# Row maxima of an attention kernel: a quarter of the tile pairs through a ScalarE Relu, the maxima turned by way of DRAM, and the output product in one piece

## The chip, the cores and the metric

The kernel runs on one core of a Trainium2 chip. The metric is device time in microseconds (us). The core has five engines that run side by side and wait for each other through semaphores: TensorE (PE in the profile, its weight loads PEld), VectorE (DVE), ScalarE (ACT), GpSimd (POOL) and SyncE (SP), which here only issues DMAs. Matmuls write to PSUM banks of 128 x 512 float32; VectorE and ScalarE read those banks, GpSimd does not.

## The reference, cut to what matters

```python
x = A_x                                                    # 2048 x 512, 32 heads of 16
mod = silu(c) @ w_mod                                      # six rows: sa, ca, ga, sb, cb, gb
h = layernorm(x) * (1 + ca) + sa
q = (h @ wq) as 32 heads; k = h @ wk; v = h @ wv           # one k and one v for all heads
p = softmax(q k^T * 16 ** -0.5)
x = x + ga * ((p v) as 2048 x 512 @ wo)
h = layernorm(x) * (1 + cb) + sb
x = x + gb * ((sigmoid(h @ w_gate) * (h @ w_up)) @ w_down)
```

The softmax is over 2048 keys for each of 32 x 2048 rows. The kernel subtracts each row's exact maximum before the exponential, so it needs the scores twice: once to find the maxima, once to exponentiate.

## The kernel before, in words

Queries come in four blocks `b` of 512, and a unit is four heads of one block: 32 units, numbered `i`. A unit has 16 steps (`kb`), one per 128 keys; `s = 16 i + kb` counts all 512 steps.

In a step `scores(n)` is called for n = 0 to 3, one head each. It issues two things. `st_tile` multiplies 128 keys by 512 queries into a PSUM bank of the tag `st` (two banks), and ScalarE takes the exponential of it into the tile `P`. `a_tile` multiplies 128 queries by 512 keys into a bank of the tag `sa` (three banks), 76 tiles ahead (`A0`, so about 19 steps, for the next unit), and VectorE reduces it to one maximum per row, in `mx`. In scores(n) the `a_tile` is that of head `n ^ 1`. A unit has 64 such tiles: 4 heads, 4 blocks `qt` of 128 queries, 4 blocks `kc` of 512 keys. The two matmuls of one scores(n) use different halves of TensorE's rows.

`pv` adds the product of the step two before (`LAG`) to the bank `c`: four matmuls with 32 columns of `V` each, in float32. In a step without feed-forward work it comes in two halves of 256 queries, one after scores(1), one after scores(3); with feed-forward work it comes whole after scores(1).

The steps of the first eight units carry, between scores(0) and scores(1), pieces of the query projection (`light`, tile `pq`: 24 pairs of matmuls over 17 steps, so one or two pairs a step, up to step 121). From unit 8 on, `plan` hands out pieces of the feed-forward layer of the block before (tiles `po`, `pgu`, `pd`), four to five pairs of matmuls per step, placed after scores(0), scores(2) and scores(3). A few steps get none.

When a unit's 64 tiles are done, `max_end`, called three steps before the unit's first scores, reduces `mx` to 16 columns (tile `m`), `max_rows` turns them on TensorE into a bank of the tag `sa`, ScalarE copies and scales that, GpSimd splits it into a high and a low float16 (`mh`), and four DMAs write it into two rows of the query tile `qp`. A constant in the key tile `kp` makes the score matmul subtract the maximum. In unit 0 the order of tiles is by blocks of queries, the maxima are turned a block at a time, and `parts` lets its steps work on one such block.

From the first step on the program order on TensorE, VectorE and ScalarE is the written order (`keep`, through `Ordered`, once `pinned` is set); GpSimd and SyncE are ordered by a scheduler. Before the first step (the prologue) the scheduler orders all engines, from the list `PLAN`.

Of the kernel before, what the change touches and what calls it, by code (L numbers as in the profile page):

```python
# [28 lines left out]
EPS = 1e-5  # L29
SH = 4.0  # L30
SW = 16.0
SM = 16.0

PLAN = 'n1 x2 l0 k0 x3 t1 l3 e1 w0 l1 n2 w3 k1 w1 q00 n3 q01 t2 t3 e2 e3 l2 m a1 k2 a2 k3 a4 w2 a8 p z3 a12 z4 a16 z2 a18 z5'

E32 = [(0, 1), (1, 1), (2, 0), (3, 3), (3, 1)]
ELO = [(0, 3), (0, 1), (3, 1), (3, 2), (2, 1), (3, 0), (1, 1)]
# [3 lines left out]
LAG = 2  # L43
# [16 lines left out]
PBUFS = 4  # L60
SBANKS = {"st": 2, "sa": 3}
GWB = 3
HBUFS = 36


@with_exitstack
def adaln_mqa_glu_kernel(
# [15 lines left out]
    pool, sp = nc.gpsimd, nc.sync  # L83
# [6 lines left out]
    cp = ctx.enter_context(tc.tile_pool(name="cp", bufs=1))  # L90
# [12 lines left out]
    def sbank(name):  # L103
        return psum["s"].tile([P, 512], F32, tag=name, name=name, bufs=SBANKS[name]) if "s" in psum else bank(name)
# [13 lines left out]
    pinned = []  # L118
# [46 lines left out]
    def t32(name, shape=(P, 512)):  # L165
        return wp.tile(list(shape), F32, tag="f32", name=name, bufs=18)
# [152 lines left out]
        dve.scalar_tensor_tensor(lo, w_, SW, hi, op0=ALU.mult, op1=ALU.subtract)  # L319


    kp = cp.tile([P, S], F16, name="kp")
    V = cp.tile([P, NKB, 32], F32, name="V")
    dve.memset(V, 1.0)
    qD = dr.tile([2, D, S], F16, name="qD")
# [58 lines left out]

# [28 lines left out]
    mxs = {}  # L413
# [3 lines left out]
    Cs = {}  # L417
# [22 lines left out]
        return qps[b, o], 2 * (u % 2)  # L440


    def a_tile(i, n):
        qp, pr0 = get_q(i)
        if i not in mxs:
            mxs[i] = wp.tile([P, 4, 4, 4], F32, tag="mx", name="mx", bufs=2)
        h = n % 4
        kc, qt = (n // 4 % 4, n // 16) if i == 0 else (n // 16, n // 4 % 4)
        j, pr = heads[h]
        sa = sbank("sa")  # L450
        pe.matmul(sa, qp[64 * j:64 * j + 64, pr0 + pr, qt * P:(qt + 1) * P],  # L451
                  kp[64 * j:64 * j + 64, kc * 512:(kc + 1) * 512], start=True, stop=True)
        dve.tensor_reduce(mxs[i][:, 2 * j + pr, qt, kc:kc + 1], sa, axis=AX.X, op=ALU.max)  # L453
        if i == 0 and n % 16 == 15:
            pend.append((i, n // 16, n // 16 + 1))
        elif i > 0 and n == 63:
            pend.append((i, 0, 4))

    pend = []

    def max_end(i, t0, t1):
        nt = t1 - t0
        n = 4 * nt
        m16 = wp.tile([P, n], F32, tag="m16", name="m16", bufs=4)
        dve.tensor_reduce(m16.rearrange("p (h t) -> p h t", t=nt), mxs[i][:, :, t0:t1, :], axis=AX.X, op=ALU.max)
        return lambda: max_rows(i, t0, t1, m16)

    def max_rows(i, t0, t1, m16):
        qp, pr0 = get_q(i)
        nt = t1 - t0  # L470
        n = 4 * nt
        pm = sbank("sa")
        pe.transpose(pm[:n, :P], m16, ident)
        mh = wp.tile([n, 2, P], F16, tag="mh", name="mh", bufs=4)
        if pinned:
            m32 = wp.tile([n, P], F32, tag="m32", name="m32", bufs=4)
# [3 lines left out]
        else:  # L480
            dve.tensor_scalar(mh[:, 0], pm[:n, :P], 1.0 / SM, None, op0=ALU.mult)
            dve.scalar_tensor_tensor(mh[:, 1], pm[:n, :P], 1.0 / SM, mh[:, 0],
                                     op0=ALU.mult, op1=ALU.subtract)
        for j in range(2):
            for h in range(2):
                r = 64 * j + 48 + h
                sp.dma_start(qp[r:r + 1, pr0:pr0 + 2, t0 * P:t1 * P], mh[2 * nt * j:2 * nt * (j + 1), h, :])


    def parts(i, t):  # L490
        if i == 0:
            return [(4 * (t % 4) + n, slice(n * P, (n + 1) * P), slice(t // 4 * P, (t // 4 + 1) * P)) for n in range(4)]
        return [(t, slice(0, QB), slice(0, QB))]

    def st_tile(i, t, pr, j):
        qp, pr0 = get_q(i)
        if j == 0:
            P_["p"] = P2.tile([P, 2, 512], F32, tag=f"P{pr}", name=f"P{pr}", bufs=PBUFS)
        p_ = P_["p"]
        s_ = sbank("st")  # L500
        for kb, cols, qs in parts(i, t):
            pe.matmul(s_[:, cols], kp[64 * j:64 * j + 64, kb * P:(kb + 1) * P],
                      qp[64 * j:64 * j + 64, pr0 + pr, qs], start=True, stop=True)
        act.activation(p_[:, j], s_, AF.Exp, scale=0.25)
        Ps[i, t, 2 * pr + j] = p_[:, j]

    def pv(i, t, half=None):
        if t == 0 and half != 1:  # L510
            Cs[i] = cbank("c")
        ps = parts(i, t)
        if half is not None:
            if i == 0:
                ps = ps[2 * half:2 * half + 2]
            else:
                cut = slice(half * QB // 2, (half + 1) * QB // 2)
                ps = [(t, cut, cut)]
        for kb, cols, qs in ps:
            for hh in range(4):  # L520
                pe.matmul(Cs[i][32 * hh:32 * hh + 32, qs], V[:, kb, :], Ps[i, t, hh][:, cols],
                          start=(kb == 0 and (i == 0 or half != 1)), stop=(kb == NKB - 1 and (i == 0 or half != 0)))
        if half == 0:
            return
        for hh in range(4):
            del Ps[i, t, hh]
        if t == NKB - 1:
            unit_end(i)
# [271 lines left out]

    for tok in PLAN.split():
        f_, args = tok[0], [int(tok[1:])] if tok[0] == "a" else [int(z) for z in tok[1:]]
        if f_ == "n":
            ln1_norm(*args)
        elif f_ == "t":
            for k in range(NDC):
                ln1_tr(args[0], k)
        elif f_ == "e":
            ln1_block(*args)
        elif f_ == "k":  # L810
            kv_block(*args)
        elif f_ == "q":
            q_group(*args).alone()
        elif f_ == "w":
            split_wq(*args)
        elif f_ == "l":
            load_wq(*args)
        elif f_ == "x":
            load_x(*args)
        elif f_ == "a":  # L820
            emit_a(4 * args[0])
        elif f_ == "m":
            for i in (4, 3, 2, 5):
                load_mod(i)
        elif f_ == "z":
            mod2(*args)
        elif f_ == "p":
            max_end(*pend.pop(0))()
    emit_a(A0)
    pctx.close()  # L830
    psum["ctx"].close()
# [95 lines left out]
    for i, (b, u) in enumerate(units):  # L927
# [4 lines left out]
        for kb in range(NKB):  # L932
# [3 lines left out]
            for z in [z for z in waits if z[0] <= s]:  # L936
                waits.remove(z)
                z[1]()
            rows = [max_end(*z) for z in late]
            an = A0 + 4 * s  # L940

            def scores(n):
# [87 lines left out]
```

## Time and profile before

| | |
|---|---|
| median of 3 runs | 1740.58 us (1739.97 to 1740.6) |
| the profiled execution | 1740.14 us, its span 1738.4 us |
| TensorE, VectorE, ScalarE, GpSimd busy | 1691.9, 1443.2, 1226.3, 605.1 us |
| prologue, up to the first exponential | 115.3 us |
| units 0 to 31, to the last exponential | 115.3 to 1590 us |
| last block's feed-forward layer | the rest, to 1738.4 us |

Times within the profile are us from the start of the span. A group's row has, after its shapes and count, the busy time, the mean ns of one, and the engine's idle time just before them. A merged row of the timeline has its start, its length, the engine, the line, the operation and how many.

Matmul ends are modelled, so starts are the better mark: a matmul that starts late has waited.

### The profile page before, as it was taken

The numbers are of one execution on the slowest core, as the hardware profiler recorded it, in microseconds if no ns is written. First come the engines' busy times: TensorE is split into PE (matmuls) and PEld (weight loads), VectorE is DVE, ScalarE is ACT, GpSimd is POOL, SyncE is SP. The second block draws the span as 40 slices with busy tenths as digits, with TensorE's granted clock in tenths as the row PEclk, the third lists the DMA queues.
The fourth block names the chain that finished last, engine by engine and source line by source line (L and its number), as shares of the span: only waits on it lengthen the run. The fifth ranks groups of instructions, "written<-read, shape, count | busy, mean of one in ns | idle before, by whom it ended". The sixth has DMA issues, their size and how long they took to land.

```text
span 1738.4 us, 35892 instructions
## 1 busy us (share of the span) xinstructions
PE 1691.9 (97%) x14467; PEld 591.1 (34%) x14467; DVE 1443.2 (83%) x2407; ACT 1226.3 (71%) x2231; POOL 605.1 (35%) x715
## 2 busy tenths in 40 slices
PE   5889999999999999999999999999999999999998
PEld 3335333333233333333333333333333333333443
DVE  8889999999998988888899898988898888841311
ACT  3338888888878777777778777777778777774100
POOL 4131445454443332332245232233255141231433
PEclk9769999999999999999999999999999999999999
DMA  7111223231100110111111110011101010011211
GB/s 262 40 47 31 95 85 106 89 110 63 51 23 26 47 49 12 33 38 41 32 41 33 33 50 20 26 47 47 36 17 57 28 57 5 30 50 55 75 60 49
DMA packets 66238, 90.94 MB, mean 52 GB/s; under 512 B 14752, under 2 KB 41376, under 8 KB 66072
## 3 DMA queue, kind: packets, MB, share of 16 engines
q1 hardware_dynamic: 66072, 88.66, 15.6%
q8 instruction: 113, 1.85, 0.4%
q14 instruction: 53, 0.43, 0.1%
HBM read 67.68 MB, written 16.22 MB: 48 GB/s over the span
## 4 chain that ended last, share of the span: by engine, by line
PE 86%; DVE 7%; ACT 2%; POOL 1%; issue 1%; DMA 1%; SPq 0%; POOLq 0%; DVEq 0%; ACTq 0%
PE c L116 27%; PE st L116 20%; PE pgu L116 12%; PE sa L116 8%; PE pd L116 5%; PE pgu L139 4%; DVE mx L116 3%; PE pd L139 2%; PE pq L116 2%; PE po L116 2%; ACT P L116 2%; PE sa L451 1%; DVE mx L453 1%; PE pmod L222 1%; PE pt L116 1%
## 5 line engine op out<-in xcount | busy, mean ns | idle before, releaser
L116 ACT ACTIVATE P<-st 128x512 f32<-128x512 f32 x2048 | 1139.2, 595 | 283.7 <-PE sa L116 250.0
L116 DVE TENSOR_REDUCE mx<-sa 128x1 f32<-128x512 f32 x1972 | 1241.2, 684 | 113.6 <-PE sa L116 108.3
L116 PE MATMUL st<-qp,kp 64*128 64x512 f16 (+1 forms) x2240 | 746.8, 362 | 7.1 <-DVE mx L453 2.4
L116 PE MATMUL sa<-kp,qp 64*128 64x512 f16 x1972 | 725.3, 382 | 0.5 <-DVE mx L116 0.5
L116 PE MATMUL c<-P,V 128*32 128x512 f32 (+2 forms) x5552 | 577.6, 492 | 2.9 <-DVE cs L116 2.9
L116 PEld LDWEIGHTS <-kp 64*128 64x128 f16 x2240 | 187.8, 94 | 500.1 <-issue 407.2
L116 PE MATMUL pgu<-h2h,gw 64*128 64x512 f16 x1344 | 242.6, 376 | 0.0
L116 PEld LDWEIGHTS <-qp 64*128 64x128 f16 x1972 | 181.8, 93 | 137.0 <-issue 51.9
L116 PEld LDWEIGHTS c<-P,V 128*32 128x32 f32 x5552 | 111.5, 108 | 192.1 <-issue 177.3
L727 POOL TENSOR_SCALAR th<-th 128x512 f32<-128x512 f32 x42 | 26.0, 619 | 335.8 <-ACT th L116 325.8
L116 PE MATMUL pgu<-h2l,gw 64*128 64x512 f16 x672 | 132.3, 376 | 0.0
L116 PEld LDWEIGHTS <-gw 64*128 64x128 f16 x2016 | 99.6, 94 | 80.7 <-issue 3.1
L424 POOL MEMSET qp<- 32x2048 f16 x32 | 57.6, 1798 | 49.3 <-PE st L116 41.6
L139 PE MATMUL pgu<-h2h,gw 128*128 128x512 f16 x224 | 66.8, 379 | 0.5 <-ACT h2h L283 0.5
L733 POOL TENSOR_TENSOR gl<-th,gh 128x512 f16<-128x512 f32 x56 | 64.8, 1157 | 4.7
L478 POOL TENSOR_SCALAR mh<-m 16x128 f16<-16x128 f32 (+1 forms) x34 | 9.8, 288 | 159.3 <-ACT m L116 159.0
L730 DVE SCALAR_TENSOR_TENSOR th<-th,pgu 128x512 f32<-128x512 f32 x14 | 9.6, 688 | 66.3 <-PE pgu L139 53.0
L248 POOL TENSOR_SCALAR wst<-wst 128x512 f32<-128x512 f32 x46 | 28.5, 620 | 102.1 <-DMA wst<-in_B_w_down_dram 27.1
L721 ACT ACTIVATE th<-pgu 128x512 f32<-128x512 f32 x14 | 8.4, 597 | 76.9 <-PE pgu L139 76.9
L116 DVE COPY u<-pgu 128x512 f32<-128x512 f32 x42 | 28.5, 679 | 35.7 <-PE st L116 19.8
L750 POOL TENSOR_TENSOR ot<-ot,gb 128x512 f32<-128x512 f32 x10 | 12.7, 1273 | 126.7 <-ACT ot L116 126.7
L590 POOL TENSOR_TENSOR raw<-raw,rb 128x512 f32<-128x512 f32 x15 | 19.1, 1273 | 102.7 <-DMA rb<-lD 84.1
(164 smaller groups left out, 1435.3 us busy)
## 6 DMA issues: line engine op xcount, KB each, us to landing
gw<-wD SPq DMA_DIRECT2D x56, 512.0 KB
wD<-gw SPq DMA_DIRECT2D x14, 512.0 KB
wm<-in_w_mod_dram SPq DMA_DIRECT2D x6, 1024.0 KB
qp<-qD SPq DMA_DIRECT2D x96, 64.0 KB
xall<-in_A_x_dram SPq DMA_DIRECT2D x4, 1024.0 KB
qD<-q SPq DMA_DIRECT2D x16, 256.0 KB
raw<-cs SPq DMA_DIRECT2D x128, 32.0 KB
xr<-in_A_x_dram SPq DMA_DIRECT2D x16, 256.0 KB
```

Of the source, the lines that this page charges most:

```text
L116: return (lambda *a, **k: keep(f_(*a, **k))) if pinned else f_
L139: pe.matmul(self.bank, l_, r_, start=(n == 0), stop=(n == self.n - 1))
L222: pe.matmul(p_[32 * k:32 * (k + 1)], cbc[:, k, :], wmods[i][:, k, :], start=True, stop=True)
L248: pool.tensor_scalar(w_, w_, SW, 0.0, op0=ALU.mult, op1=ALU.add)
L424: pool.memset(qp[j:j + 32], 0.0)
L451: pe.matmul(sa, qp[64 * j:64 * j + 64, pr0 + pr, qt * P:(qt + 1) * P], kp[64 * j:64 * j + 64, kc * 512:(kc + 1) * 512], start=True, stop=True)
L453: dve.tensor_reduce(mxs[i][:, 2 * j + pr, qt, kc:kc + 1], sa, axis=AX.X, op=ALU.max)
L478: pool.tensor_scalar(mh[:, 0], m32, 1.0, 0.0, op0=ALU.mult, op1=ALU.add)
L590: keep(pool.tensor_tensor(raw, raw, rb, op=ALU.mult))
L727: pool.tensor_scalar(th, th, 1.0, 1.0, op0=ALU.add, op1=ALU.mult)
L733: pool.tensor_tensor(lo, th, hi, op=ALU.subtract)
L750: pool.tensor_tensor(ot, ot, mods2['gb'], op=ALU.mult)
```

## The change

Keys are paired in two blocks of 512. For one head of the four (head `h == qt`), and for all four heads in unit 0, the first tile of a pair holds half the difference of the two blocks' scores, from a new key tile `kd`; ScalarE writes its doubled positive part to an SBUF tile `rl`; one step later VectorE adds `rl` to the second block's scores and takes the row maximum in one instruction (`tensor_tensor_reduce`), since max(a, b) = b + max(a - b, 0). The other three heads are reduced as before. `kd` is made in the prologue by ScalarE (one more copy of `pk` for each block) and GpSimd.

The maxima are no longer turned on TensorE: GpSimd scales and splits them, VectorE turns 32 x 32 blocks, one DMA writes them to DRAM (`mD`), and four DMAs read them into `qp`. All of unit 0's maxima are turned at once, after 64 tiles, so `parts` goes, and a step of unit 0 is like any other. And `pv` is issued whole, after scores(1), in every step. `PLAN` asks for the prologue's tiles in pairs.

```diff
-PLAN = '... k1 ... l2 m a1 k2 a2 k3 a4 w2 a8 p z3 a12 z4 a16 z2 a18 z5'
+PLAN = '... k1 ... l2 m a1 k2 a3 k3 a5 w2 a8 z3 a12 z4 a16 z2 a18 z5'
...
+        k32[b] = t32("k32")
+        act.activation(k32[b], pk, AF.Identity, scale=0.5 / (SH * SW))
         act.activation(kb, pk, AF.Identity, scale=1.0 / (SH * SW), bias=kbias)
...
+        if b % 2:
+            kb = kd[:, b // 2 * QB:(b // 2 + 1) * QB]
+            d_, o_ = k32.pop(b - 1), k32.pop(b)
+            pool.tensor_tensor(d_, d_, o_, op=ALU.subtract)
+            pool.tensor_scalar(kb, d_, 1.0, 0.0, op0=ALU.mult, op1=ALU.add)
+            for j in (32, 96):
+                pool.tensor_tensor(kb[j:j + DH], d_[j:j + DH], kb[j:j + DH], op=ALU.subtract)
...
     def a_tile(i, n):
...
+            pool.memset(mxs[i], LEAST)
-        h = n % 4
-        kc, qt = (n // 4 % 4, n // 16) if i == 0 else (n // 16, n // 4 % 4)
+        h, qt, g, second = n % 4, n // 8 % 4, n // 32, n // 4 % 2
+        kc = 2 * g + second
+        both = i == 0 or h == qt
+        differ = both and not second
+        keys = kd[...] if differ else kp[...]
-        dve.tensor_reduce(mxs[i][:, 2 * j + pr, qt, kc:kc + 1], sa, axis=AX.X, op=ALU.max)
+        m_ = mxs[i][:, 2 * j + pr, qt, kc:kc + 1]
+        if differ:
+            more[i, h] = r_ = wp.tile([P, 512], F32, tag="rl", name="rl", bufs=RBUFS)
+            act.activation(r_, sa, AF.Relu, scale=2.0)
+        elif both:
+            dve.tensor_tensor_reduce(junk, sa, more.pop((i, h)), 1.0, LEAST, ALU.add, ALU.max, m_)
+        else:
+            dve.tensor_reduce(m_, sa, axis=AX.X, op=ALU.max)
...
+    def max_end(i):
+        dve.tensor_reduce(m16.rearrange("p (h t) -> p h t", t=4), mxs[i], axis=AX.X, op=ALU.max)
+        pool.tensor_scalar(m16, m16, 1.0 / SM, 0.0, op0=ALU.mult, op1=ALU.add)
+        pool.tensor_scalar(mm16[:, 0], m16, 1.0, 0.0, op0=ALU.mult, op1=ALU.add)
+        pool.tensor_tensor(mm16[:, 1], m16, mm16[:, 0], op=ALU.subtract)
+        return lambda: max_rows(i, mm16)
...
-        pe.transpose(pm[:n, :P], m16, ident)
-            act.activation(m32, pm[:n, :P], AF.Identity, scale=1.0 / SM)
-            pool.tensor_scalar(mh[:, 0], m32, 1.0, 0.0, op0=ALU.mult, op1=ALU.add)
-            pool.tensor_tensor(mh[:, 1], m32, mh[:, 0], op=ALU.subtract)
-                sp.dma_start(qp[r:r + 1, pr0:pr0 + 2, t0 * P:t1 * P], mh[2 * nt * j:2 * nt * (j + 1), h, :])
+        dve.transpose(mt, mm16.rearrange("p l c -> p (l c)"))
+        sp.dma_start(mD, mt)
+                sp.dma_start(qp[r:r + 1, pr0:pr0 + 2, :].rearrange(...), src[l, j].unsqueeze(0))
...
-            full = now_ is not None
             if len(vq) >= LAG:
-                pv(*vq[0], None if full else 0)
+                pv(*vq.pop(0))
             for z in rows:
                 z()
             scores(2)
             if now_ == "run":
                 piece()
             scores(3)
-            if len(vq) >= LAG:
-                if not full:
-                    pv(*vq[0], 1)
-                vq.pop(0)
```

What this does to the order is seen at two places. The first is TensorE in a step of the early units, without a `pq` piece in it. Before, the two score pairs that follow one half of `c` are followed by the other half (a row with x2 is two of the four heads):

```order
L116 MATMUL c<-P_2439,V 32x256 x2
L116 MATMUL c<-P_2458,V 32x256 x2
L116 LDWEIGHTS kp
L116 MATMUL st<-qp,kp 128x512
L116 LDWEIGHTS qp
L116 MATMUL sa<-kp,qp 128x512
L116 LDWEIGHTS kp
L116 MATMUL st<-qp,kp 128x512
L116 LDWEIGHTS qp
L116 MATMUL sa<-kp,qp 128x512
L116 MATMUL c<-P_2439,V 32x256 x2
L116 MATMUL c<-P_2458,V 32x256 x2
```

Now `c` is 512 wide, and after the two pairs the next step's scores follow at once:

```order
L118 MATMUL c<-P_2092,V 32x512 x2
L118 MATMUL c<-P_2111,V 32x512 x2
L118 LDWEIGHTS kp
L118 MATMUL st<-qp,kp 128x512
L118 LDWEIGHTS qp
L118 MATMUL sa<-kp,qp 128x512
L118 LDWEIGHTS kp
L118 MATMUL st<-qp,kp 128x512
L118 LDWEIGHTS qp
L118 MATMUL sa<-kp,qp 128x512
L118 LDWEIGHTS kp
L118 MATMUL st<-qp,kp 128x512
```

So four score pairs (with what `pq` or feed-forward pieces lie among them) now stand in a row between two whole `c`, where before every two had a half of `c` behind them.

The second place is ScalarE in the same units (`P0` holds the exponentials of scores(0) and (1), `P1` those of scores(2) and (3)). Before there are exponentials only:

```order
L116 ACTIVATE P0_2395<-st_2396 128x512
L116 ACTIVATE P0_2395<-st_2406 128x512
L116 ACTIVATE P1_2416<-st_2417 128x512
L116 ACTIVATE P1_2416<-st_2423 128x512
L116 ACTIVATE P0_2439<-st_2440 128x512
L116 ACTIVATE P0_2439<-st_2448 128x512
```

Now, in every second step, a Relu (`rl`) stands among them; here it is that of head 3, between the third exponential of a step and the fourth:

```order
L118 ACTIVATE P0_3065<-st_3066 128x512
L118 ACTIVATE P0_3065<-st_3074 128x512
L118 ACTIVATE P1_3084<-st_3085 128x512
L118 ACTIVATE rl_3090<-sa_3088 128x512
L118 ACTIVATE P1_3084<-st_3092 128x512
L118 ACTIVATE P0_3098<-st_3099 128x512
```

For heads 0, 1 and 2 it stands after the second exponential, between the first and the second, and after the fourth; so it moves the exponentials behind it on ScalarE, and the banks that they release.

More of the change, by code (lines that the diff above doesn't have):

```diff
@@ L29 @@
 EPS = 1e-5
+LEAST = -3.0e38
 SH = 4.0
@@ L62 @@
 GWB = 3
+RBUFS = 4
 HBUFS = 36
@@ L322, in adaln_mqa_glu_kernel @@
     kp = cp.tile([P, S], F16, name="kp")
+    kd = cp.tile([P, S // 2], F16, name="kd")
+    k32 = {}
+    junk = cp.tile([P, 512], F16, name="junk")
     V = cp.tile([P, NKB, 32], F32, name="V")
@@ L446, in a_tile @@
             mxs[i] = wp.tile([P, 4, 4, 4], F32, tag="mx", name="mx", bufs=2)
-        h = n % 4
-        kc, qt = (n // 4 % 4, n // 16) if i == 0 else (n // 16, n // 4 % 4)
+            pool.memset(mxs[i], LEAST)
+        h, qt, g, second = n % 4, n // 8 % 4, n // 32, n // 4 % 2
+        kc = 2 * g + second
         j, pr = heads[h]
+        both = i == 0 or h == qt
+        differ = both and not second
+        keys = kd[64 * j:64 * j + 64, g * 512:(g + 1) * 512] if differ else kp[64 * j:64 * j + 64, kc * 512:(kc + 1) * 512]
@@ L450, in a_tile @@
         sa = sbank("sa")
-        pe.matmul(sa, qp[64 * j:64 * j + 64, pr0 + pr, qt * P:(qt + 1) * P],
-                  kp[64 * j:64 * j + 64, kc * 512:(kc + 1) * 512], start=True, stop=True)
-        dve.tensor_reduce(mxs[i][:, 2 * j + pr, qt, kc:kc + 1], sa, axis=AX.X, op=ALU.max)
[L454 to L457, printed above, removed]
-    pend = []
[L461 to L466, printed above, removed]
@@ L490, in parts @@
[L490 to L493, printed above, removed]
+        pe.matmul(sa, qp[64 * j:64 * j + 64, pr0 + pr, qt * P:(qt + 1) * P], keys, start=True, stop=True)
+        m_ = mxs[i][:, 2 * j + pr, qt, kc:kc + 1]
[6 more added lines that the diff above has]
+            dve.tensor_reduce(m_, sa, axis=AX.X, op=ALU.max)
@@ new lines, in a_tile @@
+        if n == 63:
+            pend.append(i)
+    more = {}
+    pend = []
+    def max_end(i):
+        m16 = wp.tile([P, 16], F32, tag="m16", name="m16", bufs=2)
+        mm16 = wp.tile([P, 2, 16], F16, tag="mm", name="mm", bufs=2)
+        dve.tensor_reduce(m16.rearrange("p (h t) -> p h t", t=4), mxs[i], axis=AX.X, op=ALU.max)
[3 more added lines that the diff above has]
+        return lambda: max_rows(i, mm16)
@@ new lines, in max_rows @@
+    def max_rows(i, mm16):
+        qp, pr0 = get_q(i)
+        mt = wp.tile([P, 32], F16, tag="mt", name="mt", bufs=2)
+        dve.transpose(mt, mm16.rearrange("p l c -> p (l c)"))
+        mD = dr.tile([P, 32], F16, tag="mD", name="mD", bufs=2)
+        sp.dma_start(mD, mt)
+        src = mD.rearrange("(b l j r t) q -> l j r t b q", b=4, l=2, j=2, r=2)
+        for j in range(2):
+            for l in range(2):
+                r = 64 * j + 48 + l
+                sp.dma_start(qp[r:r + 1, pr0:pr0 + 2, :].rearrange("o r (t b q) -> o r t b q", t=4, b=4), src[l, j].unsqueeze(0))
@@ L500, in st_tile, with pv @@
         s_ = sbank("st")
-        for kb, cols, qs in parts(i, t):
-            pe.matmul(s_[:, cols], kp[64 * j:64 * j + 64, kb * P:(kb + 1) * P],
-                      qp[64 * j:64 * j + 64, pr0 + pr, qs], start=True, stop=True)
+        pe.matmul(s_, kp[64 * j:64 * j + 64, t * P:(t + 1) * P], qp[64 * j:64 * j + 64, pr0 + pr, :], start=True, stop=True)
         act.activation(p_[:, j], s_, AF.Exp, scale=0.25)
         Ps[i, t, 2 * pr + j] = p_[:, j]
-    def pv(i, t, half=None):
-        if t == 0 and half != 1:
+    def pv(i, t):
+        if t == 0:
             Cs[i] = cbank("c")
[L512 to L524, printed above, removed]
+        for hh in range(4):
+            pe.matmul(Cs[i][32 * hh:32 * hh + 32], V[:, t, :], Ps[i, t, hh], start=(t == 0), stop=(t == NKB - 1))
         for hh in range(4):
@@ L826, in adaln_mqa_glu_kernel @@
             mod2(*args)
-        elif f_ == "p":
-            max_end(*pend.pop(0))()
+    emit_a(64)
+    turned = max_end(pend.pop())
+    emit_a(68)
+    turned()
     emit_a(A0)
@@ L938, in adaln_mqa_glu_kernel @@
                 z[1]()
-            rows = [max_end(*z) for z in late]
+            rows = [max_end(z) for z in late]
             an = A0 + 4 * s
```

15 lines of the change are left out of this document (1 added, 14 removed).

## The prediction

> **What bounds the kernel now.** I read the busy time by stage first. The stages are the end of the prologue (75 to 115.3), unit 0, units 1 to 7 (159.1 to 451.7), and units 10 to 30 (541.2 to 1545).
>
> ```profile
> core 0: us, PE busy (x) PEld busy (x) DVE busy (x) ACT busy (x) POOL busy (x), PEclk, DMA share, GB/s
> 75.00:115.30 40.30, 34.37 (x114) 9.26 (x112) 34.86 (x63) 3.61 (x7) 9.60 (x14) 0.57 0.13 40
> 115.30:159.10 43.80, 42.65 (x811) 27.80 (x808) 40.31 (x65) 36.21 (x69) 7.14 (x12) 0.92 0.04 15
> 159.10:451.70 292.60, 288.18 (x3027) 91.91 (x3023) 285.55 (x473) 252.62 (x463) 139.21 (x172) 1.00 0.27 87
> 541.20:1545.00 1003.80, 1002.86 (x8378) 331.07 (x8376) 895.07 (x1455) 781.46 (x1426) 320.71 (x364) 1.00 0.11 36
> ```
>
> In units 1 to 7 TensorE and VectorE are both 98% busy, later TensorE 100% and VectorE 89%. The change relieves VectorE and loads ScalarE, so VectorE's share suggests a gain in the early units and none later. But TensorE's share is no less, and its busy time may contain waits. So I count steps, by the exponentials (four a step) in the same stretches of the tile P:
>
> ```profile
> core 0: us, PE busy (x) PEld busy (x) ACT busy (x), PEclk, DMA share, GB/s
> 159.10:451.70 292.60, 143.16 (x1824) 36.12 (x1824) 247.96 (x449) 1.00 0.27 87
> 541.20:1545.00 1003.80, 359.46 (x2744) 53.96 (x2744) 750.59 (x1344) 1.00 0.11 36
> ```
>
> That is 112 steps of 2.61 us early and 336 of 2.99 late. Next the timeline of one late step, which has its output product whole (c, 512 wide):
>
> ```profile
> 742.29 1.06 PE L116 MATMUL c<-P,V 128*32 128x512 f32 x8
> 743.28 0.39 PE L116 MATMUL st<-qp,kp 64*128 64x512 f16 x1
> 743.71 1.08 ACT L116 ACTIVATE P<-st 128x512 f32<-128x512 f32 x2 [0.71 <-PE sa L116]
> 743.73 0.38 PE L116 MATMUL st<-qp,kp 64*128 64x512 f16 x1
> 744.59 0.38 PE L116 MATMUL st<-qp,kp 64*128 64x512 f16 x1
> 744.84 0.37 PE L116 MATMUL st<-qp,kp 64*128 64x512 f16 x1
> 745.16 1.06 PE L116 MATMUL c<-P,V 128*32 128x512 f32 x8
> 746.16 0.39 PE L116 MATMUL st<-qp,kp 64*128 64x512 f16 x1
> ```
>
> The third st of a step starts at 743.28, its exponential 0.43 later; the two exponentials end at 744.79 (743.71 + 1.08), and the st at 744.84, the next step's second, starts 0.05 after that: with two st banks it needs the one that the fourth exponential frees. Then 0.32 to c, and 1.00 to the next st. 0.43 + 1.08 + 0.05 + 0.32 + 1.00 = 2.88, exactly the 743.28 to 746.16 of this step. So a step with a whole c is a loop through ScalarE and two banks; the feed-forward pieces merely fill the time in which TensorE would wait. An early step has c in halves:
>
> ```profile
> 256.31 0.64 PE L116 MATMUL c<-P,V 128*32 128x256 f32 x8
> 256.88 0.39 PE L116 MATMUL st<-qp,kp 64*128 64x512 f16 x1
> 257.12 0.37 PE L116 MATMUL st<-qp,kp 64*128 64x512 f16 x1
> 257.30 2.21 ACT L116 ACTIVATE P<-st 128x512 f32<-128x512 f32 x4 [0.24 <-PE sa L116]
> 257.44 0.64 PE L116 MATMUL c<-P,V 128*32 128x256 f32 x8
> 258.01 0.39 PE L116 MATMUL st<-qp,kp 64*128 64x512 f16 x1
> ```
>
> Here each half (0.57, 256.31 to 256.88) runs while ScalarE empties two banks; two scores and a half take 1.13 (256.88 to 258.01), ScalarE's two exponentials 1.08. That balance is what the change touches.
>
> **The change, part by part.** The durations that it needs:
>
> ```profile
> L116 ACT ACTIVATE P<-st 128x512 f32<-128x512 f32 x2048 | 1139.2, 595 | 283.7 <-PE sa L116 250.0 <-PE pgu L116 6.8 <-PE st L116 5.0
> L116 PE MATMUL c<-P,V 128*32 128x512 f32 x2896 | 385.5, 604 | 0.0
> L116 PE MATMUL c<-P,V 128*32 128x256 f32 x2144 | 171.3, 391 | 2.9 <-DVE cs L116 2.9
> 254.94 6.14 DVE L116 TENSOR_REDUCE mx<-sa 128x1 f32<-128x512 f32 x10
> L730 DVE SCALAR_TENSOR_TENSOR th<-th,pgu 128x512 f32<-128x512 f32 x14 | 9.6, 688 | 66.3 <-PE pgu L139 53.0 <-ACT th L721 13.3
> L116 DVE TENSOR_REDUCE m<-mx 128x4 f32<-128x16 f32 x3 | 0.3, 156 | 0.0
> ```
>
> c whole in every step. A whole product is 8 records, two halves 16: 2896 / 8 = 362 steps have it whole, 2144 / 16 = 134 in halves (112 early, so 22 late ones without feed-forward work), and 16 are unit 0's. By TensorE's count it saves 2 x 0.57 - 1.00 = 0.14 a step. But the half that covered the exponentials of scores(2) and (3) is gone, and early only pq pieces fill the gap, so the loop above holds: 2.88. Early: 112 x (2.88 - 2.61) = +30. One pq pair fits into the wait: the first st follows its bank at 0.43 + 0.595 + 0.05 = 1.07 after the third, it and a piece take 0.215 each (the four pairs between 743.73 and 744.59), 1.50 of 1.56. Two pairs end at 1.72, 0.16 over; 7 of 17 steps have two, 43 in units 1 to 7: +7. Late half steps cost at least VectorE's four reductions at 0.61 (6.14 / 10), 2.45: 22 x 0.43 = +9.5. Unit 0: two steps without c at 2.45, 14 at 2.88, six double ones 0.16, two Relus (below) 0.49, 47.2 against 43.8: +3.
>
> The Relus. A unit has eight, one every second step, each as long as an exponential (0.595, and 0.49 of ScalarE's time in a row, since two end in 1.08). Heads 0, 1 and 2 put theirs where the next exponential has no bank behind it that TensorE needs soon: after the second or the first, under c (ScalarE's 0.71 idle in the row above), or after the fourth, where it delays the next step's first two, whose banks are wanted only after c. I cost these at nothing; were that cover short, each costs up to 0.49. Head 3's stands between the third and the fourth exponential, in the loop. Early: 14 x 0.49 = +7. Late, 45 steps (s = 131 to 483) get it. In the first and the last of them the fourth exponential ends at 461.85 and 1510.11 and the second st of the next step comes 0.04 and 0.28 later:
>
> ```profile
> 460.76 1.09 ACT L116 ACTIVATE P<-st 128x512 f32<-128x512 f32 x2 [0.26 <-PE sa L116]
> 461.89 0.37 PE L116 MATMUL st<-qp,kp 64*128 64x512 f16 x1
> 1509.51 0.60 ACT L116 ACTIVATE P<-st 128x512 f32<-128x512 f32 x1
> 1510.39 0.38 PE L116 MATMUL st<-qp,kp 64*128 64x512 f16 x1
> ```
>
> 33 of the 45 are like the first, 11 like the last, one has more room: 33 x 0.49 + 11 x 0.26 = +19.
>
> VectorE. A unit loses eight reductions (0.61 each), and eight others take a second operand: nearest is the 688 ns row, one operand in PSUM, one not, against 684 for a reduction. The order shows a second row behind each (the read of the accumulated maximum), which no row prices: between 0 and the 156 ns of the smallest reduction; I take 0.12. So about 4 us less per unit, worth nothing where the loop above is the bound.
>
> The maxima by way of DRAM.
>
> ```profile
> 276.24 0.22 DVE L116 TENSOR_REDUCE m<-mx 128x16 f32<-128x64 f32 x1
> 277.10 0.28 PE L116 MATMUL sa<-ident,m 128*16 128x128 f32 x1
> 278.08 2.80 SPq L487 DMA_DIRECT2D qp<-mh  x4
> 283.68 0.39 PE L116 MATMUL st<-qp,kp 64*128 64x512 f16 x1
> 303.58 0.34 SPq L578 DMA_DIRECT2D lD<-rc  x1
> 305.81 0.65 SPq L580 DMA_DIRECT2D rb<-lD  x1
> ```
>
> The turn on TensorE goes: 23 late units x 0.28 = -6 (the early ones are in the absolute count). Before, the last row's DMA is issued by 280.88 and the first st that needs the rows comes at 283.68. The new path: four small GpSimd operations (one is the next unit's memset), VectorE's turn, a write to DRAM and a read behind it (2.23 from issue to issue in the lD rows), and the same four issues (2.80). With 0.3 for each of the five small operations that is 0.22 + 1.5 + 2.23 + 2.80 = 6.8, and a landing; the new steps give 3 x 2.88 = 8.64. VectorE now waits for GpSimd at its turn, with reductions queued behind it; these find no new tile during c anyway. SyncE holds what is queued behind the read for some 2 us, weight loads and stores. All hidden if GpSimd is free; it has single operations of over 1 us, so I put +2 (0 to +46, 1.5 in each of 31 units).
>
> Prologue. From 75 to 115.3 VectorE is busy 34.86 with 63 instructions, ScalarE 3.61. Unit 0's tiles now go half to ScalarE; with some 20 pairs left then, VectorE saves 20 x 0.5 = 10. Against it: TensorE is itself busy 34.37 at clock 0.57, kd comes late through GpSimd, and all maxima of unit 0 must pass DRAM (6.8 and a landing) before the first exponential. -10 to +4, I take -5.
>
> Sum: 30 + 7 + 9.5 + 3 + 7 + 19 - 6 + 2 - 5 = +66.5, on the profiled 1740.14 (0.4 below the median of the runs): 1806.6.
>
> **The rivals.** VectorE is the bound and the change does what its share suggests: for it, 285.55 of 292.60 busy; then no st waits for ScalarE, an early step is 2 x 1.13 + 1.41 x 0.215 (pq) - 0.14 = 2.42, 112 x -0.19 = -21, Relus free, -6 - 5 + 2: 1710. Against it, 744.84. It decides from early steps under 2.61 on.
>
> ScalarE takes head 3's Relus in its idle time too, so that only the loop without them costs: 1806 - 26 = 1780. Against it, the order on ScalarE.
>
> The maxima come too late at every unit: 1806 + 44 = 1850. Against it, 1.8 us of room.
>
> TensorE's clock: early steps leave it waiting some 0.5 us in each, and the row 75 to 115.3 shows 0.57 while it worked less densely. At half clock c takes about 1.0 more: 128 steps, 1935. Against it, clock 1.00 in all rows from 159.1 on. [...]
>
> **How the numbers follow.** Forecast 0.72; Relus hidden 0.10; maxima late 0.08; VectorE the bound 0.07; clock 0.03. The forecast's own range, from the prologue's bounds, a late path of up to 10 and the Relus of the other heads, is 1790 to 1826. With the hidden Relus 1778 to 1828 leaves out under 0.2. Slower 0.91, faster 0.07, same 0.02, with 0.2% (3.5 us) about what a measurement of this kernel can tell from no change.
>
> **What the profile will show.** Right: early steps of 2.88 with the second st 0.05 after the fourth exponential, ScalarE idle during c, VectorE's share in units 1 to 7 down to about 80%, steps with head 3's Relu 0.49 longer, late steps else unchanged. Wrong: early steps near 2.4; st waiting for qp at unit starts; PEclk under 1 after unit 0; TensorE waiting for VectorE's turn of the maxima.

## The result and the profile after

The changed kernel takes 1811.58 us (median of 4, 1811.17 to 1811.83) against 1740.59: a ratio of 1.040, with an interval of 1.0386 to 1.0422. The profiled execution has a span of 1809.4 us, 71.0 more than before, at a granted clock of 0.986. Cut by the starts of the first exponentials of units 0, 1, 8 and 31, these 71 us are: 8.5 less ahead of unit 0, 4.1 more in unit 0, 44.3 more in units 1 to 7, 31.8 more in units 8 to 30, and 0.7 less behind. These are the changed kernel's rows by stage (the end of the prologue, unit 0, units 1 to 7, units 8 to 30):

```profile
core 0: us, PE busy (x) PEld busy (x) DVE busy (x) ACT busy (x) POOL busy (x), PEclk, DMA share, GB/s
75.00:106.80 31.80, 27.80 (x104) 8.23 (x102) 21.12 (x58) 14.93 (x28) 0.74 (x4) 0.55 0.03 7
106.80:154.70 47.90, 40.59 (x280) 11.12 (x280) 37.11 (x68) 38.58 (x72) 14.79 (x22) 0.96 0.12 41
154.70:491.60 336.90, 279.92 (x2090) 78.00 (x2087) 262.97 (x480) 272.43 (x512) 139.03 (x186) 1.00 0.24 76
491.60:1616.70 1125.10, 1094.12 (x8932) 357.07 (x8931) 890.06 (x1622) 926.50 (x1723) 362.23 (x464) 1.00 0.11 35
```

The exponentials (tile P) of units 1 to 7 and 10 to 30, and the output product's group:

```profile
154.70:491.60 336.90, 119.33 (x896) 17.62 (x896) 247.42 (x449) 1.00 0.24 76
587.90:1616.70 1028.80, 358.59 (x2688) 52.87 (x2688) 755.55 (x1345) 1.00 0.11 35
L118 PE MATMUL c<-P,V 128*32 128x512 f32 x4096 | 546.3, 606 | 0.0
```

A step is 336.9 / 112 = 3.01 us early (2.61 before) and 1028.8 / 336 = 3.06 late (2.99), and all 512 products are whole (4096 / 8). In units 1 to 7 VectorE falls from 285.55 us of 292.60 (98%) to 262.97 of 336.90 (78%): relieved as meant, and 44 us slower. TensorE falls from 98% to 83%, so it waits. For what, an early step shows, TensorE's rows of `st` and `c` and ScalarE's own:

```profile
269.34 1.06 PE L118 MATMUL c<-P,V 128*32 128x512 f32 x8
270.34 0.39 PE L118 MATMUL st<-qp,kp 64*128 64x512 f16 x1
270.57 0.38 PE L118 MATMUL st<-qp,kp 64*128 64x512 f16 x1
271.41 0.37 PE L118 MATMUL st<-qp,kp 64*128 64x512 f16 x1 [0.47 <-ACT P L118]
272.07 0.38 PE L118 MATMUL st<-qp,kp 64*128 64x512 f16 x1
272.38 1.07 PE L118 MATMUL c<-P,V 128*32 128x512 f32 x8
273.38 0.39 PE L118 MATMUL st<-qp,kp 64*128 64x512 f16 x1
270.76 1.65 ACT L118 ACTIVATE P<-st 128x512 f32<-128x512 f32 x3 [0.74 <-PE sa L118]
272.31 0.59 ACT L118 ACTIVATE rl<-sa 128x512 f32<-128x512 f32 x1
272.79 0.61 ACT L118 ACTIVATE P<-st 128x512 f32<-128x512 f32 x1
```

The step from 270.34 to 273.38 is 3.04 us, the prediction's 2.88 and the 0.16 of a second `pq` pair. ScalarE had been idle for 0.74 under `c`; the `st` at 271.41 waits 0.47 for the bank of the third exponential (270.76 + 0.595 + 0.05). Among the waits of the whole span (us in total, times, longest) this has 84.9 us, where before it had 2.0 in 9 times:

```profile
PE st L118 <- ACT P L118: 84.9, 199, 0.6
PE sa L118 <- DVE mx L118: 5.5, 10, 0.7
DVE mt L118 <- POOL mm L495: 27.4, 30, 2.1
```

The second shows TensorE waiting for VectorE to free a bank of `sa`. The third is the new wait on the path of the maxima, VectorE's turn (`mt`) behind GpSimd's split (`mm`). It reaches TensorE in ten or so late units; this is the step of unit 13 in which the maxima are turned, 4.0 us long instead of some 2.9:

```profile
773.56 1.16 POOL L735 TENSOR_TENSOR gl<-th,gh 128x512 f16<-128x512 f32 x1
774.80 0.20 POOL L493 TENSOR_SCALAR m<-m 128x16 f32<-128x16 f32 x1
775.46 0.22 POOL L495 TENSOR_TENSOR mm<-m,mm 128x16 f16<-128x16 f32 x1
773.01 0.22 DVE L118 TENSOR_REDUCE m<-mx 128x16 f32<-128x64 f32 x1
775.71 0.21 DVE L118 STREAM_TRANSPOSE mt<-mm 128x32 f16<-128x32 f16 x1 [1.89 <-POOL mm L495]
775.85 1.84 DVE L118 TENSOR_REDUCE mx<-sa 128x1 f32<-128x512 f32 x3
776.55 0.37 PE L118 MATMUL sa<-kp,qp 64*128 64x512 f16 x1 [0.63 <-DVE mx L118]
775.95 0.33 SPq L503 DMA_DIRECT2D mD<-mt  x1
777.40 2.84 SPq L508 DMA_DIRECT2D qp<-mD  x4
```

VectorE has its last maximum at 773.23, but GpSimd is in a feed-forward operation until 774.72 and then has four small ones; VectorE stands for 1.89 us at its turn with reductions behind it, no bank of `sa` comes free, and TensorE, whose program order is the written one, stands too: its `sa` at 776.55 waits for VectorE, and `c` behind it. The DRAM part behind it is in time: write to read 1.45 (775.95 to 777.40), four issues 2.84, and no `st` of unit 14 waits for it.

The groups of the Relu, of the add and of the read behind the add:

```profile
L118 ACT ACTIVATE rl<-sa 128x512 f32<-128x512 f32 x246 | 146.9, 597 | 0.0
L118 DVE CUSTOM_DVE_ANT_0 junk<-sa,rl 128x512 f16<-128x512 f32 x247 | 169.6, 687 | 43.7 <-PE sa L118 38.9 <-PE pgu L118 1.1 <-ACT P L118 0.4
L118 DVE DVE_READ_ACCUMULATOR2_ANT mx<- 128x1 f32 x247 | 20.6, 83 | 0.0
```

### The profile page after: what moved, and what is told of

Same layout as the page of the kernel before. It is cut to its first block, busy times and chain, and to the rows that moved or that the text cites. A ratio compares the mean times of both kernels' runs of the same rounds, so it can differ in the third digit from the quotient of the medians.

```text
span 1809.4 us, 33135 instructions
## 1 busy us (share of the span) xinstructions
PE 1676.8 (93%) x12784; PEld 558.5 (31%) x12784; DVE 1305.0 (72%) x2434; ACT 1340.0 (74%) x2481; POOL 612.8 (34%) x783
## 4 chain that ended last, share of the span: by engine, by line
PE 77%; ACT 11%; POOL 4%; issue 3%; DVE 2%; DMA 1%; SPq 0%; POOLq 0%; DVEq 0%; ACTq 0%
PE c L118 25%; PE st L118 19%; PE pgu L118 9%; ACT P L118 9%; PE sa L118 6%; PE pd L118 4%; PE pgu L141 4%; PE pd L141 2%; ACT rl L118 2%; PE pq L118 2%; PE po L118 2%; PE sa L473 1%; PE pmod L224 1%; POOL th L730 1%; PE pk L373 1%
## 5 line engine op out<-in xcount | busy, mean ns | idle before, releaser
L118 DVE TENSOR_REDUCE mx<-sa 128x1 f32<-128x512 f32 x1479 | 970.1, 686 | 237.9 <-PE sa L118 176.7
L118 PE MATMUL st<-qp,kp 64*128 64x512 f16 x2048 | 744.6, 379 | 90.1 <-ACT P L118 84.9
L118 PE MATMUL sa<-kp,qp 64*128 64x512 f16 x1726 | 639.0, 382 | 5.8 <-DVE mx L118 5.5
L118 PE MATMUL c<-P,V 128*32 128x512 f32 x4096 | 546.3, 606 | 0.0
L118 PEld LDWEIGHTS <-kp 64*128 64x128 f16 x2048 | 179.4, 94 | 543.8 <-issue 437.3
L118 PEld LDWEIGHTS <-qp 64*128 64x128 f16 x1972 | 174.4, 93 | 267.9 <-issue 201.3
L118 DVE CUSTOM_DVE_ANT_0 junk<-sa,rl 128x512 f16<-128x512 f32 x247 | 169.6, 687 | 43.7 <-PE sa L118 38.9
L118 ACT ACTIVATE rl<-sa 128x512 f32<-128x512 f32 x246 | 146.9, 597 | 0.0
L118 PEld LDWEIGHTS c<-P,V 128*32 128x32 f32 x4096 | 80.8, 108 | 152.5 <-issue 144.8
L118 PE MATMUL sa<-kd,qp 64*128 64x512 f16 x246 | 94.1, 383 | 0.0
```

What stands on the lines that cost most here:

```text
L118: return (lambda *a, **k: keep(f_(*a, **k))) if pinned else f_
```

## The experiments

All runs in one table, with the profiled span of each cut as above (us; the start of the first exponential, unit 0, units 1 to 7, units 8 to 30, the rest). A ratio is against executions of the kernel before that were measured beside the run, whose medians lie between 1740.6 and 1742.0:

```
                                 median  ratio [95%]              first  u0    1-7    8-30    rest
before                           1740.59                          115.3  43.8  292.6  1093.3  193.4
after                            1811.58 1.040 [1.0386, 1.0422]   106.8  47.9  336.9  1125.1  192.7
e1  before, c whole              1792.05 1.029 [1.0275, 1.0306]   114.9  49.6  331.5  1100.1  193.9
e2  after, half c                1773.41 1.018 [1.0166, 1.0198]   108.9  44.4  309.2  1117.3  193.1
e3  after, head 3's Relu moved   1787.65 1.027 [1.0249, 1.0284]   106.4  47.3  331.2  1106.8  192.7
e4  after, split on VectorE      1804.96 1.037 [1.0348, 1.0384]   106.2  47.9  336.5  1117.8  192.7
e6  after, Relus in unit 0 only  1790.29 1.027 [1.0259, 1.0290]   109.0  48.5  333.3  1103.8  192.8
e7  after, TensorE's turn        1812.16 1.040 [1.0385, 1.0416]   109.7  48.9  337.7  1120.6  193.0
e9  e2 and e3                    1752.66 1.0065 [1.0048, 1.0082]  108.3  42.8  303.2  1101.4  193.1
e13 e2, e3 and e4                1743.78 1.001 [1.0001, 1.0019]   108.8  42.8  303.8  1093.5  193.1
e10 e2, e4 and e6                1737.08 0.9971 [0.9959, 0.9983]  109.0  44.0  297.9  1092.2  193.1
e8  e2, e6 and e7                1733.62 0.9959 [0.9946, 0.9971]  109.9  42.7  292.5  1093.4  193.3
e12 e8 without any Relu          1738.14 0.9981 [0.9972, 0.9989]  113.7  43.1  293.0  1093.2  193.1
e14 after, c one place later     1954.67 1.1225 [1.1208, 1.1243]  108.5  48.0  331.2  1266.7  198.2
```

The first column scatters by some 3 us between kernels with the same prologue (106.4 to 109.0 in after, e2, e3, e6 and e9).

**Whole c alone (e1).** The edit to the kernel before:

```diff
-            full = now_ is not None
             if len(vq) >= LAG:
-                pv(*vq[0], None if full else 0)
+                pv(*vq.pop(0))
...
-            if len(vq) >= LAG:
-                if not full:
-                    pv(*vq[0], 1)
-                vq.pop(0)
```

> The kernel before, with one thing of the change: the four c of a step are issued whole at the first place in every step, also where no feed-forward piece is in the step. No Relu, no new path of the maxima. Theory (the prediction's: ScalarE is starved while c runs, since only two exponentials can be ahead): steps of units 1 to 7 go from 2.61 to 2.88 us with one pq and to 3.04 with two, so 112 x 0.27 + 43 x 0.16 = +37, and the late steps without a piece 22 x 0.43 = +9.5: 1740.6 + 47 = 1787 (1778 to 1792), with units 1 to 7 taking about 333 us of it instead of 293. Rival (the Relus carry the loss of units 1 to 7 and the c costs nothing, having fewer and longer matmuls): 1736 to 1743.

1792.05, 51 us above before and just over the upper bound that was expected (1792): 38.9 in units 1 to 7 (37 expected), 6.8 in units 8 to 30 (9.5), and 5.8 in unit 0, which the sum had left out. No Relu is in this kernel, so the loss of the early units is that of `c`. VectorE now has 288.15 us of work in 331.50, where 285.55 filled 292.60:

```profile
164.50:496.00 331.50, 278.68 (x2145) 78.54 (x2142) 288.15 (x473) 249.75 (x463) 139.16 (x172) 1.00 0.24 77
PE st L116 <- ACT P L116: 69.9, 152, 0.5
```

The new wait is there with its 69.9 us, without the change's other parts.

**Half c given back (e2).** The changed kernel gets back the lines that e1 takes out, and the `half` argument of `pv`.

> The changed kernel with the two half c put back in every step that has no feed-forward piece; everything else of the change stays. Theory: the whole c's 47 us come back, except where a Relu stands in the same step and stretches it: 1811.6 - 47 = 1765 (1760 to 1775), units 1 to 7 near 293 to 300 us. Rival (in units 1 to 7 Relus and c share one loss, so that taking away the c alone uncovers the Relus): 1780 to 1800. Rival (c costs nothing): 1812.

1773.41: 38 us come back, not 47, and units 1 to 7 take 309.2 where 293 to 300 was expected. Part of the rest is one step of unit 6, 7.33 us long (GpSimd, TensorE, and the stage row of the 6.8 us behind):

```profile
409.25 1.16 POOL L598 TENSOR_TENSOR al<-raw,ah 128x512 f16<-128x512 f32 x1
411.15 0.22 POOL L495 TENSOR_TENSOR mm<-m,mm 128x16 f16<-128x16 f32 x1
412.25 0.58 PE L118 MATMUL sa<-kp,qp 64*128 64x512 f16 x1 [2.73 <-DVE mx L118]
411.80:418.60 6.80, 6.36 (x39) 1.15 (x38) 4.17 (x8) 2.66 (x5) 0.00 (x0) 0.50 0.03 2
```

GpSimd is in feed-forward operations until 410.41 and then splits until 411.37; TensorE waits 2.73 us for a bank of `sa`, and the clock is granted at 0.50 for the 6.8 us that follow (the last row, in which TensorE is busy 6.36). That step and the next take 10.8 us where unit 7 has 5.4. Without it units 1 to 7 would stand at about 304, by this estimate still 11 above before, while the Relus and the new turn together cost only 5.4 there in the changed kernel (336.9 less e1's 331.5). With `c` in halves they cost more; e10 and e13 tell the two apart.

**Head 3 (e3).**

```diff
-        both = i == 0 or h == qt
+        both = i == 0 or h == (qt if qt < 3 else 0)
```

> The changed kernel with the Relu and add taken from head 3 in units 1 to 31, where it falls into the step's fourth place; the pair (head 0, query tile 3) takes it instead, so that the number of Relus and adds stays the same. Theory (a Relu between the last two exponentials of a step, with c ahead, has no slack; at the first places it only shifts): the prediction's 7 + 19 = 26 us of head 3 come back: 1785 (1780 to 1792). Rival (every Relu costs its 0.49 to 0.6 us of ScalarE wherever it stands): within 5 us of 1812.

1787.65: 24 us come back for 26 expected, 5.7 of them in units 1 to 7 (7) and 18.3 in units 8 to 30 (19), with as many Relus as before. So it is the Relu's place that costs, not their number.

**The split on VectorE (e4).**

```diff
-        pool.tensor_scalar(m16, m16, 1.0 / SM, 0.0, op0=ALU.mult, op1=ALU.add)
-        pool.tensor_scalar(mm16[:, 0], m16, 1.0, 0.0, op0=ALU.mult, op1=ALU.add)
-        pool.tensor_tensor(mm16[:, 1], m16, mm16[:, 0], op=ALU.subtract)
+        dve.tensor_scalar(mm16[:, 0], m16, 1.0 / SM, None, op0=ALU.mult)
+        dve.scalar_tensor_tensor(mm16[:, 1], m16, 1.0 / SM, mm16[:, 0], op0=ALU.mult, op1=ALU.subtract)
```

> The changed kernel with the scaling and splitting of the row maxima (three GpSimd operations ahead of the turn) done on VectorE in two operations; the turn, the DRAM tile and the reads stay. Theory (from the trace of the changed kernel: in some ten late units GpSimd stands behind feed-forward operations of 1.2 us, VectorE waits at the turn, its reductions queue, and TensorE waits 1 us for a bank; one such step is 4.0 instead of 2.9 us): about 10 us come back, 1801 (1798 to 1805), and the wait of the turn for GpSimd (27.4 us) goes. Rival (the DRAM path itself is late, so the wait stays with the tile qp): 1811. Rival (VectorE's own time bounds the steps): 1811 to 1815.

1804.96: 6.6 us come back where about 10 were expected; units 8 to 30 are 7.3 shorter, and the turn's wait is gone from the list. So the late maxima were the queue on GpSimd, not DRAM. In units 6 and 21 the turning step stays long (3.64 and 3.97 us), in the author's reading as in e13 below. In unit 12 it is 3.40, although no small operation is long there, and the cause is open.

**No Relus after unit 0 (e6)** (`both = i == 0`).

> The changed kernel with Relus and adds in unit 0 alone; in units 1 to 31 all tiles of maxima go through VectorE as before. Whole c and the DRAM path stay. Theory (the Relus at a step's first three places only shift, so with head 3's gone the rest is worth nothing either way): the time of the run with head 3 spared, 1787.7 (1781 to 1792). Rival (each Relu costs ScalarE's 0.49 us in the step's loop): three more per unit gone, 31 x 3 x 0.49 = 46 us less than that run, 1742. Rival (the Relus relieve VectorE, which is 0.87 to 0.94 busy per unit without them, and that is worth something): 1795 or more.

1790.29, in the expected range and 2.6 above e3: 2.1 more in units 1 to 7, where one step of unit 6 stalls (last section), 3.0 less in units 8 to 30, and the rest ahead of unit 1. So taking the three remaining heads' Relus out gains at most some 3 us with `c` whole: they were nearly all hidden, as the prediction had it. And VectorE, busy 289.31 of 333.30 instead of 260.37 of 331.20, loses nothing by taking the work back.

**TensorE's turn (e7).** `max_end` and `max_rows` as in the kernel before, all four query tiles at once.

> The changed kernel with the row maxima turned by TensorE as before (one transpose, ScalarE's scaling, GpSimd's split, four row DMAs) in place of VectorE's turn and the DRAM tile. Whole c and all Relus stay. Theory (the new path costs by its wait for GpSimd, about 7 us as the run with the split on VectorE gave back, and saves TensorE's turn, 23 x 0.28 = 6 us): near no change, 1811 (1807 to 1815). Rival (the DRAM round trip itself makes the rows late): well below, 1790 to 1800. Rival (the turn on TensorE was dear): 1818 or more.

1812.16, no change: units 8 to 30 gain 4.5 us, and up to the end of unit 0 it loses 3.9, much of which is the scatter of the first column. The path over DRAM, its waits for GpSimd included, was neither gain nor loss beside the old turn.

**Both large terms taken back (e9)** (the edits of e2 and e3 together).

> The changed kernel with both large terms taken back: half c in steps without a feed-forward piece, and head 3's Relus moved to head 0 at query tile 3. Theory (the two terms add up: 38 us of the half c and 24 us of head 3 as measured each alone; what is left is the prologue's gain of 8.5 us, unit 0's few, and the late maxima): 1811.6 - 38 - 24 = 1749 (1740 to 1754). Rival (with the half c the loop has no slack left for a Relu at any place): 1760 to 1773.

1752.66 against the sum's 1749. The two terms add up to within 4 us.

**The gains alone (e10; e8 with TensorE's turn; e12 without any Relu).** e10 has the edits of e2, e4 and e6; e8 those of e2, e6 and e7; e12 is e8 with `kd`, its operations and unit 0's Relus taken out.

> What the runs so far leave as the change's gains, alone: the prologue and unit 0 as changed (its Relus and one turn of all maxima), the half c kept, no Relu after unit 0, the maxima turned over DRAM with the split on VectorE. Theory, from the traces: prologue 106.3, unit 0 44.4, units 1 to 7 as before 292.6, units 8 to 30 as before less TensorE's turn 1093.3 - 6 = 1087 (to 1093 if VectorE's two extra operations show), unit 31 and the rest 192.7, outside the span 2: 1725 to 1731. Rival (VectorE, without the Relus 0.9 busy per unit, can't carry the turn and the split): 1735 to 1745.

> As the last run (half c, Relus in unit 0 alone), but the maxima are turned by TensorE as in the kernel before, in every unit, all of unit 0's at once. Theory (in units 1 to 7 VectorE is 98% busy, and its turn and split, queued among the reductions, cost the last run 5 us there; late its path gave back only 1 us; so the old turn is no dearer): units 1 to 30 as before, 1386, prologue 106 to 109, unit 0 44 to 45: 1733 to 1736. Rival (TensorE's turn costs its 0.28 us in every unit and the DRAM path is the better one): 1739 to 1742.

> The run beside this one without any Relu, add and difference of keys, in unit 0 too: of the change only one turn of all of unit 0's maxima in place of four, the order of unit 0's tiles and its whole scores are left. Theory (the prologue's 6 to 9 us come from the Relus, which take 20 reductions of 0.5 us from VectorE where it is busy 34.86 of 40.3 us): the gain goes, 1739 to 1745. Rival (they come from the one turn and the plan, or the Relus' own preparation of keys eats what they save): 1732 to 1736, no more than the run beside.

e10 hit its rival: 1737.08. In units 1 to 7 it needs 297.9, 5.3 more than before. e8, which differs from e10 in the turn alone, has before's units to the tenth (292.5 and 1093.4) and the change's gain ahead of them: 1733.62, 0.4% faster than before and the fastest of all. So the 5.3 us belong to the turn and split on VectorE. e12, at 1738.14, fell between its theory (1739 to 1745) and its rival (1732 to 1736). It shows what unit 0's Relus give: 4.5 us of the 7, since without them the first exponential starts at 113.7 instead of 109.9. The other part belongs to the one turn and the new order of unit 0.

**Everything kept but the three costs (e13)** (the edits of e2, e3 and e4).

> The change with its three costs taken out and all else kept: half c in steps without a feed-forward piece, head 3's Relus moved to head 0 at query tile 3, and the maxima split on VectorE ahead of the turn; all 248 Relus and adds and the DRAM path stay. Theory (the run with the first two stood at 1752.7; the waits for GpSimd in it are about 7 us late, as the run with the split alone gave back, and 5 us in units 2, 4 and 6): 1740.7 (1735 to 1745), so that relieving VectorE of an eighth of its reductions gives nothing in units 1 to 30, since ScalarE and TensorE need as long there. Rival (with VectorE relieved and nothing in its way the early steps fall under 2.45 us): 1722 to 1732, less than the run with Relus in unit 0 alone, 1733.6.

1743.78, in the expected range and a tie with before (ratio 1.0001 to 1.0019). With 248 Relus doing an eighth of its work and all their forecast costs out of the way, units 8 to 30 take 1093.5 us (before 1093.3) and units 1 to 7 303.8, 11 more than before. The 5 us that were to come back in units 2, 4 and 6 did not: e9 had 303.2. Two runs split the 11. e10 is this kernel without the Relus of units 1 to 31, and takes 297.9: so about 6 of the 11 are the Relus, now at the three first places alone. (In units 8 to 30 they cost 1.3.) The other 5, which e10 has too, are the turn, whose steps in units 2, 4 and 6 are 4.56, 3.72 and 3.67 us long here. In unit 2:

```profile
229.52 2.27 POOL L252 TENSOR_TENSOR gw<-wst,gw 128x512 f16<-128x512 f32 x2
229.72 0.98 DVE L118 TENSOR_SCALAR mm<-m 128x16 f16<-128x16 f32 x1
230.74 1.08 DVE L118 SCALAR_TENSOR_TENSOR mm<-m,mm 128x16 f16<-128x16 f32 x1
```

These two operations on 16 elements take 0.30 and 0.25 us on average over 31 units. Here each ends 0.03 us after the GpSimd operation beside it (230.67 and 231.79). The Relus' share shows as more steps of 2.77 to 2.99: 34 of 112, where before has 16. Which engine holds those steps no run has told apart; ScalarE is busy 89% and TensorE 97% of these units, so neither has much room for work that VectorE gives up.

**One whole c, elsewhere (e14).** The changed kernel, with `c` behind the third pair of scores and its piece:

```diff
-            if len(vq) >= LAG:
-                pv(*vq.pop(0))
             for z in rows:
                 z()
             scores(2)
             if now_ == "run":
                 piece()
+            if len(vq) >= LAG:
+                pv(*vq.pop(0))
             scores(3)
```

> The changed kernel with the whole c of each step issued after the third pair of scores instead of after the second; nothing else is moved. Theory (the loop is the four exponentials less two ahead, plus c, and does not depend on where in the step the one whole c stands; only the head whose Relu falls into the loop changes): 1811, between 1800 and 1822, units 1 to 7 near 330 to 340 us. Rival (the place of c beside the pieces is what costs): below 1790 or above 1830.

Half of the theory held. In units 1 to 7 the time is 331.2, in the expected band, the plain step again 2.88, and the step that costs 0.49 more is now that of another head; a second `pq` pair no longer costs its 0.16 (the step from 269.39 to 272.27 has two and takes 2.88), since it now stands where TensorE waits. But units 8 to 30 take 142 us more than in the changed kernel, 1954.67 in all, as the rival had it (above 1830). A late step:

```profile
656.15 0.38 PE L118 MATMUL st<-qp,kp 64*128 64x512 f16 x1
656.56 0.37 PE L118 MATMUL st<-qp,kp 64*128 64x512 f16 x1
656.78 0.39 PE L118 MATMUL pgu<-h2h,gw 64*128 64x512 f16 x2
656.99 0.39 PE L118 MATMUL pgu<-h2l,gw 64*128 64x512 f16 x2
657.32 1.06 PE L118 MATMUL c<-P,V 128*32 128x512 f32 x8
658.32 0.39 PE L118 MATMUL st<-qp,kp 64*128 64x512 f16 x1
```

The piece of feed-forward work (`pgu`) now stands between the last `st` that a free bank allows and `c`. From `st` to `c` it is 0.76 (656.56 to 657.32), where the prediction's loop has 0.32: the piece, two pairs of matmuls at the prediction's 0.215, lies in the loop. Over the 368 steps of units 8 to 30, 142 us are 0.39 each, about one such piece. In the changed kernel the pieces stand where TensorE waits for a bank anyway. So the length of the loop does not depend on where `c` is, but whether the pieces are free does.

## Why the prediction was right

Forecast 1806 and measured 1811.6, in the range, by the mechanism that it gave. Point by point:

- **c whole in every step**: forecast 37 early and 9.5 late, measured alone (e1) 38.9 and 6.8. The early step is 2.88 or 3.04, as in the prediction. The late term went by VectorE's 2.45 for steps in halves, and was 2.7 too high.
- **Head 3's Relus**: forecast 7 and 19, measured (e3) 5.7 and 18.3. The other heads' Relus were costed at nothing; with `c` whole, e6 against e3 bears that out. With `c` in halves it would not have held: e13 against e10 has them at about 6 us early.
- **Unit 0**: forecast +3, measured +4.1; whole `c` alone makes it 5.8 longer in e1, so parts of the change cancel here, and the agreement of this small term is not an explanation.
- **Maxima by way of DRAM**: this was mis-sized. The sum had -6 for TensorE's turn and +2 for a late path. The late path cost about 7 (e4), and the turn was worth 0.2 a unit, not 0.28, by one unit: the turning step of unit 10 is 3.22 us before and 3.02 in e6, so some 23 x 0.2 = 4.6. The step of the prediction that failed is the sentence that the reductions queued behind VectorE's wait "find no new tile during c anyway": they wait for up to 2.1 us, `c` takes 1.0, and TensorE runs out of `sa` banks. The GpSimd operations of over 1 us were named, and then priced too low.
- **Prologue**: forecast -5 between -10 and +4, measured -8.5 in this profile, and -6 to -9 in other kernels with the same prologue. Unit 0's Relus bring the first exponential forward by 3.8 us (e8 against e12), about half of it, where the prediction had VectorE save 10.
- **Rivals**: VectorE as the bound would have left no `st` waiting; there are 199 such waits. Head 3's Relus hidden: e3 gave 24 us for them. Maxima late at every unit: ten or so of 31, and behind GpSimd, not behind the transfer. TensorE at half clock: the rows show 1.00 in units 1 to 7, though TensorE waits 17% of that time. In one late unit of the changed kernel the clock did drop, for 3.4 us (from 973.9).
- **Signs of being wrong**: two of those named did show, in small. TensorE waited for VectorE behind its turn (10 waits, 5.5 us), and the clock was once under 1.00 after unit 0. Both are small beside the terms of the loop.

The forecast's terms, read in the order of the stages, were +24.5 for units 8 to 30 and +44 for units 1 to 7; the trace has 31.8 and 44.3. The 7 us of the late stage are the wait for GpSimd, and e4, which removes it, stands at 1117.8 - 1093.3 = 24.5. That this is the forecast to the tenth is partly luck: measured alone, whole `c` was 2.7 and head 3's Relus 0.7 smaller than forecast, the gain from the turn 1.4 smaller, and e4 keeps a few long turning steps of its own.

## What to carry to other kernels

Where one engine's results come back through two banks, look for the loop (score, exponential, bank, score) before the busy shares: a block of matmuls that is put whole into that loop, or a piece of work put between the last allowed score and that block, lengthens every step, although no work is added. Here a whole `c` in place of two halves made early steps 0.35 longer on average (e1's 38.9 over 112 steps), and a piece of 0.43 in the wrong place made late ones 0.39 longer. An engine at 98% need not be worth relieving, when the engine that takes the work stands in the same loop: in units 1 to 7 VectorE has 290.57 us of work in e10 and 268.06 in e13, whose Relus took over the rest, and they are 6 us longer (297.9 to 303.8). And price a short chain over a third engine by the longest operation that can be ahead of it in that engine's queue, with all that is queued behind the waiting instruction: in unit 13 one GpSimd operation of 1.16 us and four small ones became 1.89 us at the turn and 0.63 on TensorE.

## What was not expected of the hardware

Two small VectorE operations in SBUF lasted until the GpSimd operation beside them had ended: in e13's rows above the 128x16 scaling takes 0.98 us and the split behind it 1.08, against 0.30 and 0.25 on average, and each ends 0.03 us after a GpSimd operation (of 1.16 us on average). What ties them together no run here shows. The reductions from PSUM show no such stretch (in the changed kernel 686 ns on average, 694 at most).

A single stall can cost more than itself. In e2 no matmul started for 3.1 us (409.14 to 412.25), and 6.8 us at clock 0.50 followed; in e6 none for 2.1 us (from 435.0), and 3.4 us at 0.50 followed (its units 1 to 7 have 0.99 on average); in e9 none for 2.8 us (from 403.7), and the clock stayed at 1.00, which is also the average of its units 1 to 7. In the changed kernel 3.4 us at 0.50 followed (from 973.9) although no pause between matmul starts there was over 1.1 us; in the 3.5 us ahead TensorE was busy 2.24. So clock 0.50 followed a pause of 1.1 us, and did not follow one of 2.8; what decides it no run here shows.

VectorE's read of the accumulated maximum took 83 ns in 247 cases (0.12 had been taken), and a Relu of 128x512 from PSUM 597, like an exponential (599 in the same profile).

Left open: a third bank for `st` in place of one of `sa` would test the loop of two banks directly; no run has it.
